# A fused attention and mixture-of-experts kernel: gate work of the last unit at lower steps of the first routed slot, and planning by one scan over one combined number

## The chip, the cores and the metric

The kernel runs on 1 core of one Trainium2 chip. The metric is the device time of one execution in microseconds (us). The engines are TensorE (PE), VectorE (DVE), ScalarE (ACT), GpSimd (POOL) and SyncE (SP), which here only issues transfers.

## The reference

Three stages run one after the other; the change touches the passage from the second to the third.

```python
x = attention(q, k, v, w_phi)                    # 4608 tokens x 512
h = x @ w_in; x1 = (h * cos(h)) @ w_out          # dense stage
logits = x1 @ w_gate + modality_bias[modality_id]
e_idx = argmax(logits, axis=1)                   # one of 8 experts per token
gate_w = softmax(logits)[token, e_idx]
for e in range(8):                               # routed stage
    mask = e_idx == e
    out[mask] = gate_w[mask, None] * (relu(x1[mask] @ w1[e]) @ w2[e])
```

## The kernel before

**Dense stage.** The 4608 tokens go in 9 units of 512, and a unit runs 16 steps. Every float32 operand is split in a high and a low part, and a product is three matmuls. For the last two units the result x1T (512 features by 512 tokens) is gated on TensorE: `logits(u,d)` splits a quarter d of x1T on DVE and POOL (x1h, x1l), and its returned function `pe` does two matmuls into `pl`; after the fourth quarter ACT copies `pl` out (lsb). `rows(u,c)` transposes 128 tokens (pr) and writes them to x1d in memory. `route1(u)` turns the logits (pt) into one-hot rows ob. `route2(u)` ranks every token within its expert (matmuls pk) and writes one record (token, weight) per token into the table `tab` by four scatters on POOL (L601), each of which waits for the one before. The table has a region of REG rows for each expert.

**Routed stage.** Tokens of one expert are worked off in slots of 256 (`body`). A slot needs its records (mrec, loaded by SP from `tab`, L713), its rows of x1 (xg, two gathers on POOL, L715), and its expert's weights: 8 loads of 512 KB into raw tiles (`fetch`, L690 and L691, on SP), each split in two casts by ACT (high part, L697) and two subtractions by DVE (low part, L698). `body(i)` has 12 steps: 4 steps of 24 matmuls mh, each followed by hh on ACT and hl on DVE, and 8 steps of 6 matmuls po, in two halves of 24. `finish` scales a half on ACT (o) and writes it out by an indirect transfer on POOL (L788). `prep(i)` transposes slot i's rows (px) and splits them to xT; `hooks` puts it behind step 9 of the slot before.

**The place of the change.** Slots 0 and 1 use the expert that has the most tokens before the last unit, so they can start before the last unit is routed. The rest of the gate work of unit 8 (the last) is put between the steps of slot 0, by the table given to `run`: after step n, its entries run. `order` then plans all later slots from the final counts: a slot's expert (ie), its offset in `tab` (io) and the numbers of full and half slots (ni), by small operations on one partition of DVE. SP reads ie and io into registers (L613, called by `load_e` and `load_off`) before it loads records and weights. `tokens(2)` is the load of slot 2's records and its gathers, `weights(8,12)` its first four weight loads (raw_8, raw_9, raw_10 and raw_0); the others are issued from the hooks of slot 1.

**What sets the order.** Each engine runs its instructions in one fixed order. A scheduler chooses it when the program is built, from the program's steps and its own estimates of durations; the table sets the program order, and the scheduler may move work of other tiles past it. SP's queue is in order as well: what stands behind the record load waits for it. Buffers are shared by tag: "row" turns among kvt, kvt and qt; "fr" is kt, "n" is qt.

The table before:

```python
    run(body(0,0),{0:[lambda:lg(0)(u)],1:[lambda:pe(u),lambda:lg(1)(u)],2:[lambda:pe(u),lambda:lg(2)(u)],3:[lambda:pe(u),lambda:lg(3)(u)],
             4:[lambda:rows(u,0)],5:[lambda:pe(u),lambda:rows(u,1)],6:[lambda:rows(u,2)],7:[lambda:rows(u,3),lambda:route1(u)],
             9:[lambda:route2(u)],10:[lambda:prep(1)],11:[order,lambda:tokens(2),lambda:load_e(2),lambda:load_e(3),lambda:weights(8,12)]})
```

Of the kernel before, what the change touches and what calls it, by code (L numbers as in the profile page):

```python
# [296 lines left out]
def gate_consts(tc, ctx, cpool, ps, ident, modality_id, modality_bias, w_gate, wgt):  # L297
    nc=tc.nc
    C={}
    with tc.tile_pool(name="g_tmp",bufs=1) as tp:  # L300
# [31 lines left out]

        sl=tp.tile([1,25],I32,name="sl"); nc.gpsimd.iota(sl,pattern=[[1,25]],base=0,channel_multiplier=0)
        slot=cpool.tile([1,25],F32,name="slot"); nc.vector.tensor_copy(slot,sl)

        tok=cpool.tile([P,4,9],I32,name="tok")
        nc.gpsimd.iota(tok[:,:,0:4],pattern=[[1152,4],[1,4]],base=0,channel_multiplier=4)
# [14 lines left out]
        nc.vector.tensor_tensor(bt,mf.unsqueeze(2).to_broadcast([P,36,8]),mb[:,1:2,:].to_broadcast([P,36,8]),ALU.mult)  # L352
        nc.vector.tensor_tensor(b0,mz.unsqueeze(2).to_broadcast([P,36,8]),mb[:,0:1,:].to_broadcast([P,36,8]),ALU.mult)
        nc.vector.tensor_tensor(bt,bt,b0,ALU.add)
    C.update(g1=g1,g2=g2,fold=fold,tri=tri,one=one,rev=rev,run=run,base=base,tok=tok,bt=bt,num=num,slot=slot,pool=cpool)
    return C


def moes(tc, ctx, consts, S, ps, ident, att, end_att, xt, w_in, w_out, x1d, tab, wgt, w1, w2, out):
# [10 lines left out]
    def xtile(tag,name,dt=F32R):  # L370
        if tag=="x1T": return late[0].tile([P,512],dt,tag="x1T",name=name,bufs=4)
        if tag=="row": return S(turn(("kvt","kvt","qt"),tag),name,dt)
        return S({"fr":"kt","n":"qt","gh":"kvh","gl":"kvl"}[tag],name,dt)
# [149 lines left out]
    lsb={}; pls={}  # L523
    def logits(u,d):

        h=xtile("row",f"x1h_{u}_{d}"); l=xtile("row",f"x1l_{u}_{d}")
        nc.vector.tensor_copy(h,x1T[u,d])
        nc.gpsimd.tensor_tensor(l,x1T[u,d],f32(h),ALU.subtract)
        def pe():
            if d==0: pls[u]=ms(f"pl_{u}")  # L530
            pl=pls[u]
            nc.tensor.matmul(pl[0:16,:],C["g1"][:,d,:],h,start=d==0,stop=False)
            nc.tensor.matmul(pl[0:16,:],C["g2"][:,d,:],l,start=False,stop=d==3)
            if d==3:
                t=xtile("row",f"lsb_{u}",F32)
                nc.scalar.copy(t[0:16,:],pl[0:16,:])
                lsb[u]=t[0:16,:]
        return pe
# [16 lines left out]
    def small(n,u,shape,dt=F32): return sb.tile(shape,dt,tag="s_"+n,name=f"{n}_{u}",bufs=1)  # L555
# [71 lines left out]
    def order():  # L627
# [4 lines left out]
        srt=small("srt",0,[1,8]); nc.vector.max(srt,t)  # L632
        ki=small("ki",0,[1,8],I32); nc.vector.tensor_copy(ki,srt)
        ei=small("ei",0,[1,8],I32); nc.vector.tensor_scalar(ei,ki,7,None,op0=ALU.bitwise_and)
        e=small("oe",0,[1,17]); nc.vector.memset(e[:,16:17],0.0)
        nc.vector.tensor_copy(e[:,0:8],ei); nc.vector.tensor_copy(e[:,8:16],ei)
        nc.vector.tensor_scalar(ki,ki,0xffff,None,op0=ALU.bitwise_and)
        n=small("on0",0,[1,16])
        for j,more in ((0,T//2-1),(1,T-1)):
# [1 line left out]
            nc.vector.tensor_scalar(kj,kj,11,None,op0=ALU.logical_shift_right)  # L641
            nc.vector.tensor_copy(n[:,8*j:8*j+8],kj)
        nc.vector.tensor_tensor(n[:,8:16],n[:,8:16],n[:,0:8],ALU.subtract)
        b=small("ob",0,[1,17]); nc.vector.tensor_scalar(b,e,float(REG),None,op0=ALU.mult)
        nc.vector.scalar_tensor_tensor(b[:,8:16],n[:,0:8],float(T),b[:,8:16],op0=ALU.mult,op1=ALU.add)
        end=n
        for i in (1,2,4,8):
            t2=small(f"on{i}",0,[1,16]); nc.vector.tensor_copy(t2[:,0:i],end[:,0:i])
            nc.vector.tensor_tensor(t2[:,i:16],end[:,i:16],end[:,0:16-i],ALU.add)
            end=t2  # L650
        de=small("de",0,[1,16]); nc.vector.tensor_tensor(de,e[:,1:17],e[:,0:16],ALU.subtract)
        do=small("do",0,[1,16]); nc.vector.tensor_tensor(do,b[:,1:17],b[:,0:16],ALU.subtract)
        nc.vector.scalar_tensor_tensor(do,n,-float(T),do,op0=ALU.mult,op1=ALU.add)
        ge=small("ge",0,[1,NS1,16])
        ie=small("ie",0,[1,NS1],I32); io=small("io",0,[1,NS1],I32)
        se=small("se",0,[1,NS1]); so=small("so",0,[1,NS1])
        for d_,s_ in ((de,se),(do,so)):
            nc.vector.tensor_tensor(ge,C["slot"].unsqueeze(2).to_broadcast([1,NS1,16]),end.unsqueeze(1).to_broadcast([1,NS1,16]),ALU.is_ge)
            nc.vector.tensor_tensor(ge,ge,d_.unsqueeze(1).to_broadcast([1,NS1,16]),ALU.mult)
            nc.vector.tensor_reduce(s_,ge,AX.X,ALU.add)  # L660
        nc.vector.tensor_scalar(ie,se,e[:,0:1],None,op0=ALU.add)
        nc.vector.scalar_tensor_tensor(so,C["slot"],float(T),so,op0=ALU.mult,op1=ALU.add)
        nc.vector.tensor_scalar(io,so,b[:,0:1],None,op0=ALU.add)

        ni=small("ni",0,[1,2+NSH],I32)
        nc.vector.tensor_copy(ni[:,0:1],end[:,7:8]); nc.vector.tensor_copy(ni[:,1:2],end[:,15:16])
# [122 lines left out]
    def run(steps,hooks):  # L789

        n=0
        for _ in steps:
            for f in hooks.get(n,()): f()
            n+=1
        for f in hooks.get("end",()): f()
# [4 lines left out]
    def lg(d):  # L800
        def f(u): pend.append(logits(u,d))
        return f
    def pe(u): pend.pop(0)()
# [52 lines left out]
    def tokens(i):  # L856
        if i<NS0+2: alloc_g(i)
        load_off(i); gather(i)
    def weights(m0,m1):
        for m in range(m0,m1): fetch(m)  # L860
    run(body(0,0),{0:[lambda:lg(0)(u)],1:[lambda:pe(u),lambda:lg(1)(u)],2:[lambda:pe(u),lambda:lg(2)(u)],3:[lambda:pe(u),lambda:lg(3)(u)],
             4:[lambda:rows(u,0)],5:[lambda:pe(u),lambda:rows(u,1)],6:[lambda:rows(u,2)],7:[lambda:rows(u,3),lambda:route1(u)],
             9:[lambda:route2(u)],10:[lambda:prep(1)],11:[order,lambda:tokens(2),lambda:load_e(2),lambda:load_e(3),lambda:weights(8,12)]})
    def hooks(i,steps):


# [117 lines left out]
```

## Time and profile before

| What | us |
|---|---|
| median of 3 runs (1785.21 to 1790.61) | 1786.19 |
| the profiled execution | 1787.86 |
| its span in the trace | 1786.2 |
| TensorE busy | 1721.5 (96%) |
| DVE busy | 1243.0 (70%) |
| ACT busy | 931.2 (52%) |
| POOL busy | 640.0 (36%) |

TensorE is busy in 96% of the span. The page's slices show where it isn't: in the first part of the span, in two short stretches between 1260 and 1350 us (the passage from the dense to the routed stage), and at the end. A wait of another engine costs nothing as long as TensorE has work. "At 1331.26" means 1331.26 us after the start of the span.

### The profile page before, as it was taken

To read this page: it belongs to the slowest core of one execution; us is meant where nothing else is said; L and a number is where in the kernel's file an instruction comes from. 1 tells how busy PE (TensorE), PEld (TensorE's weight loads), DVE (VectorE), ACT (ScalarE), POOL (GpSimd) and SP (SyncE) were. 2 spreads that over 40 slices of the span, in tenths; PEclk is the share of its full clock that TensorE was granted. 3 is DMA by queue.
4 is the path that set the end of the run, shared out by engine and by line. 5 is a ranking of instruction groups with operands and counts; after the bars stand their busy time and mean duration, and the time that the engine had idled before them with its cause. 6 is when DMAs were issued, how large, how long until landed. Compare 5 with 4: busy or idle time off the path is not lost. (4 is left out here: it accounts for less than half of the span.)

```text
span 1786.2 us, 27417 instructions
## 1 busy us (share of the span) xinstructions
PE 1721.5 (96%) x9818; PEld 1481.6 (83%) x9818; DVE 1243.0 (70%) x2366; ACT 931.2 (52%) x1694; POOL 640.0 (36%) x496
## 2 busy tenths in 40 slices
PE   8999999998889999999999999999889999999986
PEld 7999999997668888888888888888778999999975
DVE  6878877779896586868586868574547565666555
ACT  5777777776554343434343434343427555565555
POOL 0544544546654233434333333343322221111121
PEclk9999999999899999999999999999999999999998
DMA  6334333332332010101010101000329775766666
GB/s 177 101 112 125 90 100 105 87 95 98 119 112 78 12 36 12 36 12 36 12 36 13 36 13 36 13 1 24 118 83 389 236 236 198 258 220 222 221 222 221
DMA packets 144614, 194.37 MB, mean 109 GB/s; under 512 B 64967, under 2 KB 89671, under 8 KB 144466
## 3 DMA queue, kind: packets, MB, share of 16 engines
q1 hardware_dynamic: 136514, 170.93, 30.3%
q0 software_dynamic: 7952, 21.54, 3.6%
q8 instruction: 83, 1.36, 0.3%
q14 instruction: 65, 0.53, 0.1%
HBM read 162.70 MB, written 30.51 MB: 108 GB/s over the span
## 5 line engine op out<-in xcount | busy, mean ns | idle before, releaser
L455 PE MATMUL ph<-x,w 128*128 128x512 f32 x1728 | 427.9, 396 | 10.3 <-DVE fr L474 9.0
L455 PEld LDWEIGHTS ph<-x,w 128*128 128x128 f32 x1728 | 325.8, 190 | 88.3 <-DVE fr L474 12.2
L477 POOL TENSOR_TENSOR gl<-fr,gh 128x512 fp32r<-128x512 f32 x144 | 215.0, 1495 | 397.4 <-DVE gh L476 329.6
L698 DVE TENSOR_TENSOR m<-raw,m 128x512 fp32r<-128x512 f32 x336 | 219.2, 694 | 134.0 <-ACT m L697 131.8
L487 PE MATMUL acc<-w,gh 128*128 128x512 f32 x896 | 276.3, 390 | 0.0
L697 ACT CAST m<-raw 128x512 fp32r<-128x512 f32 x336 | 195.6, 618 | 70.8 <-PE mh L738 31.4
L468 ACT ACTIVATE n<-ph 128x512 int32<-128x512 f32 x144 | 85.8, 596 | 263.9 <-PE ph L455 260.9
L738 PEld LDWEIGHTS mh<-xT,m 128*128 128x128 f32 x1728 | 211.3, 193 | 4.9 <-ACT xT L724 2.3
L738 PE MATMUL mh<-xT,m 128*128 128x256 f32 x1728 | 212.5, 284 | 2.3 <-ACT xT L724 1.8
L487 PEld LDWEIGHTS acc<-w,gh 128*128 128x128 f32 x896 | 168.8, 188 | 35.0
L470 DVE SCALAR_TENSOR_TENSOR fr<-ph,n 128x512 f32<-128x512 f32 x144 | 99.1, 688 | 134.9 <-ACT n L468 114.6
L487 PE MATMUL acc<-w,gl 128*128 128x512 f32 x448 | 175.2, 392 | 6.8 <-POOL gl L477 6.8
L750 PE MATMUL po<-m,hh 128*128 128x512 f32 x576 | 181.2, 396 | 0.0
L517 DVE SCALAR_TENSOR_TENSOR junk<-x1T,wg 128x512 f32<-128x512 f32 x224 | 180.1, 804 | 0.0
L471 ACT ACTIVATE fr<-fr 128x512 f32<-128x512 f32 x144 | 91.1, 633 | 160.3 <-DVE fr L470 159.7
L168 PEld LDWEIGHTS kv<-v,ke 128*128 128x128 f32 (+1 forms) x1280 | 146.4, 191 | 13.0 <-issue 7.1
L168 PE MATMUL kv<-v,ke 128*128 128x65 f32 (+1 forms) x1280 | 152.0, 273 | 1.7 <-ACT ke L148 1.6
L474 DVE SCALAR_TENSOR_TENSOR fr<-fr,ph 128x512 f32<-128x512 f32 x144 | 98.6, 685 | 74.5 <-ACT fr L472 74.3
L788 POOL DMA_INDIRECT out_dram<-o,mrec x39 | 39.5, 1014 | 292.9 <-ACT o L787 253.4
L223 PE MATMUL pn<-qx,kvz 128*128 128x288 f32 x512 | 136.3, 409 | 3.2 <-DVE xo L230 3.0
L750 PEld LDWEIGHTS po<-m,hh 128*128 128x128 f32 x576 | 106.1, 190 | 20.2
L223 PEld LDWEIGHTS pn<-qx,kvz 128*128 128x128 f32 x512 | 92.6, 191 | 24.7 <-DVE xo L230 3.7
(210 smaller groups left out, 2940.8 us busy)
## 6 DMA issues: line engine op xcount, KB each, us to landing
raw<-in_moe_w_dram SPq DMA_DIRECT2D x179, 512.0 KB
xt<-xo SPq DMA_DIRECT2D x16, 576.0 KB
xr<-xt SPq DMA_DIRECT2D x36, 256.0 KB
raw_k<-in_k_dram SPq DMA_DIRECT2D x32, 256.0 KB
raw_q<-in_q_dram SPq DMA_DIRECT2D x32, 256.0 KB
v<-in_v_dram SPq DMA_DIRECT2D x64, 128.0 KB
st<-in_moe_w_in_dram SPq DMA_DIRECT2D x16, 512.0 KB
st<-in_moe_w_out_dram SPq DMA_DIRECT2D x16, 512.0 KB
```

Source lines behind the costliest of these rows:

```text
L168: nc.tensor.matmul(o,e[p0:p1,idx*256+s*F:idx*256+(s+1)*F],vh[p0:p1,h,cc,:],start=first and h==0 and s==0,stop=last,skip_group_check=True)
L223: nc.tensor.matmul(pn,kz[:,s,h*P:(h+1)*P],qx[:,h,s,su],start=s==0,stop=s==1)
L455: nc.tensor.matmul(ph,A[:,ws],xhl[u,d][k],start=n[0]==0,stop=n[0]==11); n[0]+=1
L470: nc.vector.scalar_tensor_tensor(g,ph,INV2PI,n,op0=ALU.mult,op1=ALU.subtract)
L474: nc.vector.scalar_tensor_tensor(g,g,-0.5,ph,op0=ALU.add,op1=ALU.mult)
L477: nc.gpsimd.tensor_tensor(gl,g,f32(gh),ALU.subtract)
L487: nc.tensor.matmul(accs[u][c],A[:,ws],B,start=(f==0 and k==0),stop=(f==NF-1 and k==2))
L517: return lambda: tc.keep_in_program_order(nc.vector.scalar_tensor_tensor(junk,x1T[u,c],1.0,wg[e],op0=ALU.mult,op1=ALU.mult,accum_out=lgs[u ...
L697: nc.scalar.copy(h,a)
L698: nc.vector.tensor_tensor(l,a,f32(h),ALU.subtract)
L738: nc.tensor.matmul(ph[:,f2*T:(f2+1)*T],A[:,ws],B[d//2][:,xs],start=n==0,stop=n==11); n+=1
L750: nc.tensor.matmul(po[c],A[:,ws],B,start=(f==0 and j==0),stop=(f==NF2-1 and j==2))
```

## The change

The gate work of unit 8 moves to lower steps: all four splits after step 0, all eight gate matmuls after step 2, `route1` after step 3 (before: 7), `route2` after step 6 (before: 9), `order` after step 7, and the record, expert and weight loads of slot 2 after step 8 (before: 11). Three of the four splits get buffers of the tags "fr" and "n". In `order`, the expert and the offset of a slot become one number (8 times the offset plus the expert), so that one compare, multiply and sum over 25 x 16 numbers gives both; a mask and a shift take them apart. The doubling steps of the running sum become one scan.

```diff
--- before.py
+++ after.py
@@ -332,6 +332,7 @@
 
         sl=tp.tile([1,25],I32,name="sl"); nc.gpsimd.iota(sl,pattern=[[1,25]],base=0,channel_multiplier=0)
         slot=cpool.tile([1,25],F32,name="slot"); nc.vector.tensor_copy(slot,sl)
+        ones=cpool.tile([1,16],F32,name="ones"); nc.vector.memset(ones,1.0)
 
         tok=cpool.tile([P,4,9],I32,name="tok")
         nc.gpsimd.iota(tok[:,:,0:4],pattern=[[1152,4],[1,4]],base=0,channel_multiplier=4)
@@ -352,7 +353,7 @@
         nc.vector.tensor_tensor(bt,mf.unsqueeze(2).to_broadcast([P,36,8]),mb[:,1:2,:].to_broadcast([P,36,8]),ALU.mult)
         nc.vector.tensor_tensor(b0,mz.unsqueeze(2).to_broadcast([P,36,8]),mb[:,0:1,:].to_broadcast([P,36,8]),ALU.mult)
         nc.vector.tensor_tensor(bt,bt,b0,ALU.add)
-    C.update(g1=g1,g2=g2,fold=fold,tri=tri,one=one,rev=rev,run=run,base=base,tok=tok,bt=bt,num=num,slot=slot,pool=cpool)
+    C.update(g1=g1,g2=g2,fold=fold,tri=tri,one=one,rev=rev,run=run,base=base,tok=tok,bt=bt,num=num,slot=slot,ones=ones,pool=cpool)
     return C
 
 
@@ -523,7 +524,8 @@
     lsb={}; pls={}
     def logits(u,d):
 
-        h=xtile("row",f"x1h_{u}_{d}"); l=xtile("row",f"x1l_{u}_{d}")
+        th,tl=("fr","n") if u==NU-1 and d<3 else ("row","row")
+        h=xtile(th,f"x1h_{u}_{d}"); l=xtile(tl,f"x1l_{u}_{d}")
         nc.vector.tensor_copy(h,x1T[u,d])
         nc.gpsimd.tensor_tensor(l,x1T[u,d],f32(h),ALU.subtract)
         def pe():
@@ -632,8 +634,6 @@
         srt=small("srt",0,[1,8]); nc.vector.max(srt,t)
         ki=small("ki",0,[1,8],I32); nc.vector.tensor_copy(ki,srt)
         ei=small("ei",0,[1,8],I32); nc.vector.tensor_scalar(ei,ki,7,None,op0=ALU.bitwise_and)
-        e=small("oe",0,[1,17]); nc.vector.memset(e[:,16:17],0.0)
-        nc.vector.tensor_copy(e[:,0:8],ei); nc.vector.tensor_copy(e[:,8:16],ei)
         nc.vector.tensor_scalar(ki,ki,0xffff,None,op0=ALU.bitwise_and)
         n=small("on0",0,[1,16])
         for j,more in ((0,T//2-1),(1,T-1)):
@@ -641,26 +641,22 @@
             nc.vector.tensor_scalar(kj,kj,11,None,op0=ALU.logical_shift_right)
             nc.vector.tensor_copy(n[:,8*j:8*j+8],kj)
         nc.vector.tensor_tensor(n[:,8:16],n[:,8:16],n[:,0:8],ALU.subtract)
-        b=small("ob",0,[1,17]); nc.vector.tensor_scalar(b,e,float(REG),None,op0=ALU.mult)
-        nc.vector.scalar_tensor_tensor(b[:,8:16],n[:,0:8],float(T),b[:,8:16],op0=ALU.mult,op1=ALU.add)
-        end=n
-        for i in (1,2,4,8):
-            t2=small(f"on{i}",0,[1,16]); nc.vector.tensor_copy(t2[:,0:i],end[:,0:i])
-            nc.vector.tensor_tensor(t2[:,i:16],end[:,i:16],end[:,0:16-i],ALU.add)
-            end=t2
-        de=small("de",0,[1,16]); nc.vector.tensor_tensor(de,e[:,1:17],e[:,0:16],ALU.subtract)
-        do=small("do",0,[1,16]); nc.vector.tensor_tensor(do,b[:,1:17],b[:,0:16],ALU.subtract)
-        nc.vector.scalar_tensor_tensor(do,n,-float(T),do,op0=ALU.mult,op1=ALU.add)
+
+        b=small("ob",0,[1,17]); nc.vector.memset(b[:,16:17],0.0)
+        nc.vector.tensor_scalar(b[:,0:8],ei,8.0*REG+1.0,None,op0=ALU.mult)
+        nc.vector.scalar_tensor_tensor(b[:,8:16],n[:,0:8],8.0*T,b[:,0:8],op0=ALU.mult,op1=ALU.add)
+        end=small("on1",0,[1,16])
+        nc.vector.tensor_tensor_scan(end,C["ones"],n,0.0,op0=ALU.mult,op1=ALU.add)
+        db=small("db",0,[1,16]); nc.vector.tensor_tensor(db,b[:,1:17],b[:,0:16],ALU.subtract)
+        nc.vector.scalar_tensor_tensor(db,n,-8.0*T,db,op0=ALU.mult,op1=ALU.add)
         ge=small("ge",0,[1,NS1,16])
-        ie=small("ie",0,[1,NS1],I32); io=small("io",0,[1,NS1],I32)
-        se=small("se",0,[1,NS1]); so=small("so",0,[1,NS1])
-        for d_,s_ in ((de,se),(do,so)):
-            nc.vector.tensor_tensor(ge,C["slot"].unsqueeze(2).to_broadcast([1,NS1,16]),end.unsqueeze(1).to_broadcast([1,NS1,16]),ALU.is_ge)
-            nc.vector.tensor_tensor(ge,ge,d_.unsqueeze(1).to_broadcast([1,NS1,16]),ALU.mult)
-            nc.vector.tensor_reduce(s_,ge,AX.X,ALU.add)
-        nc.vector.tensor_scalar(ie,se,e[:,0:1],None,op0=ALU.add)
-        nc.vector.scalar_tensor_tensor(so,C["slot"],float(T),so,op0=ALU.mult,op1=ALU.add)
-        nc.vector.tensor_scalar(io,so,b[:,0:1],None,op0=ALU.add)
+        nc.vector.tensor_tensor(ge,C["slot"].unsqueeze(2).to_broadcast([1,NS1,16]),end.unsqueeze(1).to_broadcast([1,NS1,16]),ALU.is_ge)
+        nc.vector.tensor_tensor(ge,ge,db.unsqueeze(1).to_broadcast([1,NS1,16]),ALU.mult)
+        sv=small("sv",0,[1,NS1+8])[:,0:NS1]; nc.vector.tensor_reduce(sv,ge,AX.X,ALU.add)
+        nc.vector.scalar_tensor_tensor(sv,C["slot"],8.0*T,sv,op0=ALU.mult,op1=ALU.add)
+        iv=small("iv",0,[1,NS1],I32); nc.vector.tensor_scalar(iv,sv,b[:,0:1],None,op0=ALU.add)
+        ie=small("ie",0,[1,NS1],I32); nc.vector.tensor_scalar(ie,iv,7,None,op0=ALU.bitwise_and)
+        io=small("io",0,[1,NS1],I32); nc.vector.tensor_scalar(io,iv,3,None,op0=ALU.logical_shift_right)
 
         ni=small("ni",0,[1,2+NSH],I32)
         nc.vector.tensor_copy(ni[:,0:1],end[:,7:8]); nc.vector.tensor_copy(ni[:,1:2],end[:,15:16])
@@ -858,9 +854,9 @@
         load_off(i); gather(i)
     def weights(m0,m1):
         for m in range(m0,m1): fetch(m)
-    run(body(0,0),{0:[lambda:lg(0)(u)],1:[lambda:pe(u),lambda:lg(1)(u)],2:[lambda:pe(u),lambda:lg(2)(u)],3:[lambda:pe(u),lambda:lg(3)(u)],
-             4:[lambda:rows(u,0)],5:[lambda:pe(u),lambda:rows(u,1)],6:[lambda:rows(u,2)],7:[lambda:rows(u,3),lambda:route1(u)],
-             9:[lambda:route2(u)],10:[lambda:prep(1)],11:[order,lambda:tokens(2),lambda:load_e(2),lambda:load_e(3),lambda:weights(8,12)]})
+    run(body(0,0),{0:[lambda:[lg(d)(u) for d in range(4)]],2:[lambda:[pe(u) for d in range(4)]],3:[lambda:route1(u)],
+             4:[lambda:rows(u,0)],5:[lambda:rows(u,1)],6:[lambda:route2(u),lambda:rows(u,2)],7:[lambda:rows(u,3),order],
+             8:[lambda:tokens(2),lambda:load_e(2),lambda:load_e(3),lambda:weights(8,12)],10:[lambda:prep(1)]})
     def hooks(i,steps):
 
 
```

Three places show how instructions move. The first is TensorE in slot 0, around the last step of mh (pl is the gate matmul, pr a transposition for x1d). Before:

```order
L738 MATMUL mh_0_3_12131<-xT_0_1_11985,m0_7_11797 128x256 x3
L532 MATMUL pl_8_12089<-x1h_8_2_12127,g1_591 16x512
L533 MATMUL pl_8_12089<-x1l_8_2_12128,g2_592 16x512
L750 MATMUL po_0_0_12166<-m1_0_11798,hh_0_0_12052 128x512 x2
L750 MATMUL po_0_0_12166<-m1_0_11798,hl_0_0_12053 128x512
L750 MATMUL po_0_0_12166<-m1_1_11799,hh_0_0_12052 128x512 x2
L750 MATMUL po_0_0_12166<-m1_1_11799,hl_0_0_12053 128x512
L542 MATMUL pr_8_0_12174<-ident_60,x1T_8_0_12012 128x128
```

Now:

```order
L534 MATMUL pl_8_12132<-x1h_8_0_12058,g1_591 16x512
L535 MATMUL pl_8_12132<-x1l_8_0_12059,g2_592 16x512
L534 MATMUL pl_8_12132<-x1h_8_1_12062,g1_591 16x512
L535 MATMUL pl_8_12132<-x1l_8_1_12063,g2_592 16x512
L534 MATMUL pl_8_12132<-x1h_8_2_12066,g1_591 16x512
L535 MATMUL pl_8_12132<-x1l_8_2_12067,g2_592 16x512
L534 MATMUL pl_8_12132<-x1h_8_3_12070,g1_591 16x512
L535 MATMUL pl_8_12132<-x1l_8_3_12071,g2_592 16x512
L734 MATMUL mh_0_3_12143<-xT_0_0_11986,m0_1_11793 128x256 x3
```

All eight gate matmuls now stand in a row ahead of the last step of mh; before, the third pair stood behind it and the fourth later still.

The second is POOL behind the last split x1l (tab is the scatter of records, out_0_dram a slot's result, xg a gather). Before:

```order
L528 TENSOR_TENSOR x1l_8_3_12163<-x1T_8_3_12018,x1h_8_3_12162 128x512
L788 DMA out_0_dram<-o_0_0_12220,mrec_0_11771 4608x512
L601 DMA tab_67<-rec_8_12257,pi_8_12294 38912x2 x2
L788 DMA out_0_dram<-o_0_1_12326,mrec_0_11771 4608x512
L601 DMA tab_67<-rec_8_12257,pi_8_12294 38912x2 x2
L715 DMA xg_2_0_12399<-x1d_66,mrec_2_12398 128x512
```

Now:

```order
L530 TENSOR_TENSOR x1l_8_3_12071<-x1T_8_3_12020,x1h_8_3_12070 128x512
L603 DMA tab_67<-rec_8_12196,pi_8_12257 38912x2
L784 DMA out_0_dram<-o_0_0_12277,mrec_0_11773 4608x512
L603 DMA tab_67<-rec_8_12196,pi_8_12257 38912x2 x3
L784 DMA out_0_dram<-o_0_1_12397,mrec_0_11773 4608x512
L711 DMA xg_2_0_12347<-x1d_66,mrec_2_12346 128x512
```

The first scatter now stands ahead of slot 0's first output write, and the second output write behind all four scatters.

The third is ACT from slot 1's first hh on (m2 are the split weights of slot 2's second product, raw the loaded ones, o a scaled result). Before:

```order
L740 ACTIVATE hh_1_0_12442<-mh_1_0_12417 128x512
L740 ACTIVATE hh_1_1_12492<-mh_1_1_12467 128x512
L740 ACTIVATE hh_1_2_12521<-mh_1_2_12496 128x512
L740 ACTIVATE hh_1_3_12550<-mh_1_3_12525 128x512
L697 CAST m2_0_11806<-raw_8_12024 128x512
L697 CAST m2_1_11807<-raw_8_12024 128x512
L697 CAST m2_2_11808<-raw_9_12025 128x512
L697 CAST m2_3_11809<-raw_9_12025 128x512
L697 CAST m2_4_11810<-raw_10_12026 128x512
L697 CAST m2_5_11811<-raw_10_12026 128x512
L697 CAST m2_6_11812<-raw_0_11782 128x512
L787 ACTIVATE o_1_0_12595<-po_1_0_12554,mrec_1_11777 128x512
```

Now:

```order
L736 ACTIVATE hh_1_0_12427<-mh_1_0_12402 128x512
L736 ACTIVATE hh_1_1_12477<-mh_1_1_12452 128x512
L693 CAST m2_0_11808<-raw_8_12026 128x512
L693 CAST m2_1_11809<-raw_8_12026 128x512
L693 CAST m2_2_11810<-raw_9_12027 128x512
L693 CAST m2_3_11811<-raw_9_12027 128x512
L736 ACTIVATE hh_1_2_12506<-mh_1_2_12481 128x512
L693 CAST m2_4_11812<-raw_10_12028 128x512
L693 CAST m2_5_11813<-raw_10_12028 128x512
L693 CAST m2_6_11814<-raw_0_11784 128x512
L736 ACTIVATE hh_1_3_12535<-mh_1_3_12510 128x512
```

hh_1_2 and hh_1_3 of slot 1 now stand behind casts of slot 2's weights. DVE has the same new order, with hl_1_2 and hl_1_3 behind the low parts of these casts.

## Rows read from the trace of the kernel before

**Rows 1.** Busy us by stretch: PE, PEld, DVE, ACT, POOL; clock, DMA, GB/s

```profile
1270.00:1275.00 5.00, 2.53 (x6) 2.05 (x7) 4.55 (x6) 4.50 (x8) 2.40 (x2) 0.70 1.02 369
...
1335.00:1340.00 5.00, 0.00 (x0) 0.00 (x0) 2.59 (x4) 2.63 (x5) 0.96 (x1) 0.68 1.04 370
1340.00:1345.00 5.00, 3.20 (x11) 2.72 (x12) 2.80 (x5) 3.35 (x7) 1.33 (x2) 0.50 1.05 396
1345.00:1350.00 5.00, 5.00 (x25) 4.29 (x25) 5.00 (x9) 4.95 (x11) 2.31 (x2) 0.79 1.04 393
```

**Rows 2.** Timeline of PE: start, us, engine, line, operation [idle before, releaser]

```profile
1340.48 0.48 PE L723 MATMUL px<-ident,xg 128*128 128x128 f32 x1 [7.92 <-DMA xg<-x1d,mrec]
...
1342.27 1.75 PE L723 MATMUL px<-ident,xg 128*128 128x128 f32 x7 [1.31 <-DMA xg<-x1d,mrec]
...
1348.09 11.78 PE L738 MATMUL mh<-xT,m 128*128 128x256 f32 x96
```

**Rows 3.** Timeline of POOL: the last unit's four scatters, an output write

```profile
1310.48 0.98 POOL L601 DMA_INDIRECT tab<-rec,pi  x1 [2.55 <-DVE ki L633]
1315.56 0.96 POOL L601 DMA_INDIRECT tab<-rec,pi  x1 [4.10 <-DMA tab<-rec,pi]
1316.82 0.98 POOL L788 DMA_INDIRECT out_dram<-o,mrec  x1 [0.30 <-issue]
1321.76 0.96 POOL L601 DMA_INDIRECT tab<-rec,pi  x1 [3.96 <-DMA tab<-rec,pi]
1326.52 0.96 POOL L601 DMA_INDIRECT tab<-rec,pi  x1 [3.79 <-DMA tab<-rec,pi]
```

**Rows 4.** Timeline of the SP queue: the load of slot 2's records

```profile
1331.26 0.39 SPq L713 DMA_DIRECT2D mrec<-tab  x1
```

**Rows 5.** Waits of the SP queue, 1290-1480: us in total, times, longest

```profile
SPq L613 <- DVE ie L661: 11.0, 1, 11.0
SPq L713 <- DMA tab<-rec,pi: 10.6, 1, 10.6
```

**Rows 6.** Timeline of PE and its weight loads in slots 0 and 1

```profile
1298.31 0.60 PE L542 MATMUL pr<-ident,x1T 128*128 128x128 f32 x4
...
1298.66 0.71 PE L750 MATMUL po<-m,hh 128*128 128x512 f32 x2
...
1308.63 0.12 PEld L587 LDWEIGHTS <-tri 128*128 128x128 bf16 x2 [0.26 <-DVE s L576]
...
1310.46 1.03 PE L723 MATMUL px<-ident,xg 128*128 128x128 f32 x8
...
1326.97 0.61 PE L750 MATMUL po<-m,hh 128*128 128x512 f32 x2
...
1327.65 0.61 PE L750 MATMUL po<-m,hh 128*128 128x512 f32 x2
```

**Rows 7.** Timeline of ACT: last hh of slot 1, then slot 2's casts

```profile
1324.42 0.60 ACT L740 ACTIVATE hh<-mh 128x512 fp32r<-128x512 f32 x1 [2.28 <-PE mh L738]
1335.92 1.14 ACT L697 CAST m<-raw 128x512 fp32r<-128x512 f32 x2 [10.90 <-DMA raw<-in_moe_w_dram]
1337.61 1.14 ACT L697 CAST m<-raw 128x512 fp32r<-128x512 f32 x2 [0.56 <-DMA raw<-in_moe_w_dram]
...
1342.44 0.62 ACT L697 CAST m<-raw 128x512 fp32r<-128x512 f32 x1 [1.65 <-DMA raw<-in_moe_w_dram]
1342.96 0.68 ACT L787 ACTIVATE o<-po,mrec 128x512 f32<-128x512 f32 x1
```

**Rows 8.** Timeline of DVE: last planning step; low part of raw_0's first cast

```profile
1319.90 0.22 DVE L663 TENSOR_SCALAR io<-so,ob 1x25 int32<-1x25 f32 x1
...
1343.09 0.69 DVE L698 TENSOR_TENSOR m<-raw,m 128x512 fp32r<-128x512 f32 x1 [1.50 <-ACT m L697]
```

**Rows 9.** Timeline of POOL in unit 7: first and last of its four scatters

```profile
1246.25 0.99 POOL L601 DMA_INDIRECT tab<-rec,pi  x1 [0.15 <-DVE kmi L620]
...
1258.53 0.96 POOL L601 DMA_INDIRECT tab<-rec,pi  x1 [2.97 <-DMA tab<-rec,pi]
```

## The prediction

> **What bounds the kernel now.** I read the busy time of the engines in stretches first. Outside the first routed slots TensorE is full, so only a stretch where it idles can give time back. The last such stretch before the steady routed slots is at 1332 to 1347 us: TensorE does no work in one whole 5 us stretch, and its granted clock is 0.50 (1.2 GHz) in the next [rows 1]. The timeline of PE shows what it waits for: the transposes px of slot 2 wait 7.92 us and once more 1.31 us for the gather of x1 rows, and slot 2 itself starts at 1348.09 [rows 2]. I followed the gather backwards. POOL sends the record table of the last unit in four scatters, each only after the one before has landed [rows 3]; SP loads slot 2's records right after the fourth, at 1331.26 [rows 4]; and the list of waits of SP says that this load waited 10.6 us for the table alone, long after the planning numbers were there [rows 5]. The weight loads of slot 2 stand behind that load on SP, so they too are counted from it. I call this moment M; it is 1331.26 before.
>
> **The change, step by step.** *Gate earlier.* Count back from the rank matmuls pk, which began at 1308.63 [rows 6]. Between their old and their new place lie 18 matmuls po at 0.227 us (three start 0.68 us after three others), two groups of four transposes at 0.35 us from start to next start, and one pair of gate matmuls, about the size of two po: 4.08 + 0.70 + 0.46 = 5.2 us; the wait of 0.26 us ahead of pk goes as well [rows 6], since ob is then ready before. So pk begins near 1303.1. From pk to the first scatter took 1.85 us [rows 3, 6], so the first scatter is at 1305.0, 5.5 us earlier. The eight gate matmuls in a row need all four splits x1l. These now have buffers of their own and no longer wait for a matmul, and POOL has nothing else to do there; I count no wait. Without that cover each microsecond late costs one in M.
>
> *Scatters.* The order on POOL also changes: before, an output write stood between scatters 2 and 3; now one stands between 1 and 2, another behind 4. The interval with an output write 1.3 us behind the scatter was 6.20 us; the other two intervals on POOL were 5.08 and 4.76, and scatter 4 to SP's load 4.74 [rows 3, 4]. I take 6.20 + 4.76 + 4.76 + 4.74 = 20.5 us, since SP waits for the landing and not for POOL; M is then 1325.4, 5.9 us earlier. Bounds: in unit 7, four scatters began within 12.28 us, 4.09 each [rows 9], which gives M = 1321.4; 6.20 for each gives 1329.8. The Trainium skill (DMA: Bandwidth & Descriptors, section "Two DMAs through the same engine are not ordered") says that descriptors of one queue on one engine start in order; by that a write behind a scatter should not hold it up, M would be 1.4 us earlier and the end too, 1783.7. The 6.20 row speaks against it.
>
> *Planning.* Of the two compare, multiply and sum groups one goes, the doubling steps become one scan, and a mask and a shift that split the combined number are added. From pk to the last planning step DVE took 1308.63 to 1320.12, other work included [rows 6, 8]. I cost all of it at nothing: SP's load still waited 10.6 us for the table after the numbers were there [rows 5]. Even at its old length, 11.5 us, planning that begins with pk at 1303.1 ends at 1314.6, 11 us before the new M. Only without that cover would the shorter planning count, with some part of the 11.5.
>
> *What is moved along.* SP has the same order of loads as before, so the loads come at the old distances from M: raw_9 at M + 6.35 and raw_0 at M + 11.18, read from ACT's casts, which began when the loads landed [rows 7]. Nothing else on SP is passed.
>
> *The new wait.* The order shows what the diff doesn't. Before, ACT had all four hh of slot 1 ahead of slot 2's casts and did the last at 1324.42, then idled 10.90 us for raw_8 [rows 7]. Now hh_1_2 stands behind the four casts of raw_8 and raw_9, and hh_1_3 behind those of raw_10 and half of raw_0; DVE is in the same order. TensorE needs hh_1_2 after only 12 of slot 1's 48 po. These began about 1324.1, just before the last hh, and 0.3 us of waiting is gone, so that is at 1324.1 - 0.3 + 2.7 = 1326.5. That ACT doesn't pass over a waiting cast can be seen before: the output o of slot 1's first half ran at 1342.96, right behind the cast that had waited for raw_0, though its matmuls had been done since about 1330 [rows 7]. The Trainium skill (TensorE: Matmul & The Clock Gate, section "Architectural detail: the array is 16× 32×32, not 1× 128×128") calls the queues of ACT and DVE strict FIFO, which the o row agrees with; it is the rule that speaks against this change. If they were not, rival E below would be the result.
>
> So TensorE's wait for the gather is exchanged for a wait for weights, with more matmuls still to do behind it. hh_1_2: 1325.4 + 6.35 + 1.14 + 0.60 = 1333.5, so PE idles some 7 us from 1326.5. hh_1_3: raw_0 lands at 1336.6, its cast takes 0.62 and hh 0.60; on DVE the low part of that cast comes 0.65 us behind the cast's start and takes 0.69 [rows 7, 8], and hl_1_3 of the same shape as much again: 1336.6 + 0.65 + 0.69 + 0.69 = 1338.6. From there: 4 po, 12 po, the transposes px (1.03 us at full clock for slot 1's eight [rows 6]), 12 po: 28 x 0.227 + 1.03 = 7.4, so 1346.0. The clock: in the stretch from 1270, where PE resumed at 1272.5, the granted clock is 0.70, so 1.2 GHz for some 3 us; after px at 1342.27 it was at that level until about 1347.1, 4.8 us [rows 1, 2]. A second, short idle ends at 1337.8; 1.2 GHz from there for 0.8 to 4.8 us costs 0 to 2.0 us, and I take 1.0 (about 3 us, as at 1272). **Slot 2 starts at 1347.0 instead of 1348.09: a gain of 1.1 us.**
>
> Is slot 2 ready then? Behind raw_0 five more loads of 512 KB and 512 KB of gathers must land; at 396 GB/s [rows 1] that is 7.9 us, 1344.5; then two casts (1.14) and xT's first cast (0.62, as a raw cast of its shape): 1346.3 on ACT, 1347.0 with DVE's 0.69 [rows 7, 8]. It just fits. From then on TensorE is full as before, so the difference is carried to the end. The profiled execution took 1787.86 us with a span of 1786.2, and the median of the timed runs is 1786.19; I put the difference on the median: 1786.19 - 1.1 = 1785.1.
>
> **The rivals.** *B, faster: the scatters go at unit 7's pace.* M = 1321.4, the end 4.1 us earlier still: 1781.0. For it: the pace of 4.09 [rows 9]; against it: all four intervals of this very unit were longer [rows 3]. *E, faster: the casts don't hold hh up.* Then PE reaches px at 1332 and waits for the gather, at M + 9.2 and M + 11.0 (from rows 2 and 4), until 1336.4; with 12 po and the clock it could start slot 2 at 1341, but the last weights of its first matmuls land and are split only near 1343.4: a gain of 4.7, 1781.5. The order of ACT speaks against it. *C, slower: the loads of slot 3 hold slot 2 up.* hh_2_0 now stands behind eight casts for slot 3, before behind two. Behind raw_0 eight loads and 1 MB of gathers must land for that, 13.2 us at the rate above, 1349.8; two casts, hh and hl (2.4 us) bring 1352.2, and PE needs that at 1352.7, after 48 matmuls mh of slot 2. So it decides from a landing after 1350.3, and each microsecond later costs one. With these loads 5 us late (at 285 GB/s, say) PE idles 4.5 us, and with the clock at half after it loses 2 more: 1786.19 - 1.1 + 6.5 = 1791.6. Against it: before, the casts for slot 3 found their data there. *D, no change of the gate's time:* the gate matmuls wait for POOL or DVE and the first scatter stays at 1310.48. Then M is 5.5 us later than reckoned, and 1.1 us gained becomes 4.4 lost: 1790.6.
>
> **How the numbers follow.** About 0.3% (5.4 us) is what a measurement of this kernel can tell from no change. Forecast A, the exchange of one wait for another, 0.74; B 0.08; E 0.06; C 0.07; D 0.05. Faster by over 0.3% (under 1780.8) are about half of B and E and the lower end of A, with the clock soon back and a short interval each: 0.10. Slower by over 0.3% (over 1791.6) are most of C and a little of D and A: 0.08. Within 0.3%: 0.82. The range goes from B's time, 1781.0, to 6.20 us for three more scatter intervals less a little (M at 1329): 1789.5.
>
> **What would show it.** In the changed profile: the first scatter near 1305 and the four intervals; SP's record load near 1325.4; the list of waits with po waiting for hh on PE, and px no longer waiting for the gather; ACT's hh of slot 1 broken into two early and two late ones at 1333 and 1337; slot 2's first mh near 1347. The forecast is wrong if hh_1_2 runs before 1330, if the record load is not 4 us or more earlier, or if TensorE idles again in slot 2.

## The result: slower, by work that the diff doesn't touch

The changed kernel takes 1799.43 us (median of 4 runs, 1797.05 to 1800.62), the kernel before 1786.51 beside it: a ratio of 1.0066, 95% interval 1.0054 to 1.0078. The forecast was 1785.1 within 1781.0 to 1789.5; the time lies outside, on the other side. The profiled execution took 1797.05 us, with a span of 1795.3, 9.1 more than before (the medians differ by 12.9); the readings below are of it. One execution of a later kernel (slot 1's hh first, again) took 4448.44 us, for a cause that isn't known, and is left out of that kernel's ratio.

The changed passage does about what was forecast. The loss is elsewhere: the first matmul of routed slot 0, which stands ahead of every moved step, begins at 1289.12 instead of 1282.10. Lining up the 9818 matmuls of both traces one by one shows where the time goes: +1.5 us by the end of the attention, +7.0 by the end of the dense stage, +6.6 where slot 3 begins, +9.5 at the last matmul. So it is lost bit by bit in all three stages, and none in the passage that was changed.

### The profile page after: what moved, and what is told of

Read it like the earlier page. It is cut to its first block, busy times and chain, and to the rows that moved or that the text cites. A ratio compares the mean times of both kernels' runs of the same rounds, so it can differ in the third digit from the quotient of the medians.

```text
span 1795.3 us, 27417 instructions
## 1 busy us (share of the span) xinstructions
PE 1732.0 (96%) x9818; PEld 1481.8 (83%) x9818; DVE 1238.0 (69%) x2355; ACT 931.7 (52%) x1694; POOL 641.4 (36%) x496
## 5 line engine op out<-in xcount | busy, mean ns | idle before, releaser
L746 PE MATMUL po<-m,hl 128*128 128x512 f32 x288 | 114.0, 396 | 0.0
```

The source lines that it names most:

```text
L746: nc.tensor.matmul(po[c],A[:,ws],B,start=(f==0 and j==0),stop=(f==NF2-1 and j==2))
```

## The profile after

TensorE's share of the span is the 96% of before, and its busy time is longer:

```profile
span 1795.3 us, 27417 instructions
PE 1732.0 (96%) x9818; PEld 1481.8 (83%) x9818; DVE 1238.0 (69%) x2355; ACT 931.7 (52%) x1694; POOL 641.4 (36%) x496
```

A full engine can still do less. This is the list of groups for PE between 700 and 1100 us, in the dense stage (line, operation, shapes, count; busy us, mean ns of one; idle before), of the changed kernel:

```profile
L456 PE MATMUL ph<-x,w 128*128 128x512 f32 x864 | 211.6, 393 | 0.2
L488 PE MATMUL acc<-w,gh 128*128 128x512 f32 x575 | 179.2, 392 | 0.0
L488 PE MATMUL acc<-w,gl 128*128 128x512 f32 x287 | 112.7, 393 | 0.0
```

Together 1726 matmuls in 400 us. The same list before has 1743, at 389 to 391 ns:

```profile
L455 PE MATMUL ph<-x,w 128*128 128x512 f32 x867 | 211.9, 391 | 0.2
L487 PE MATMUL acc<-w,gh 128*128 128x512 f32 x584 | 179.8, 389 | 0.0
L487 PE MATMUL acc<-w,gl 128*128 128x512 f32 x292 | 113.6, 389 | 0.0
```

The granted clock is 1.00 there in both. On POOL, the first scatter of one unit and of the fifth unit after it, in the changed kernel and then before:

```profile
671.90 1.46 POOL L603 DMA_INDIRECT tab<-rec,pi  x1 [0.18 <-issue]
...
1116.93 1.25 POOL L603 DMA_INDIRECT tab<-rec,pi  x1
```

```profile
669.80 1.45 POOL L601 DMA_INDIRECT tab<-rec,pi  x1 [0.18 <-issue]
...
1110.64 1.25 POOL L601 DMA_INDIRECT tab<-rec,pi  x1 [0.15 <-issue]
```

(1116.93 - 671.90) / 5 = 89.0 us per unit; before it was (1110.64 - 669.80) / 5 = 88.2. The rate isn't the same through a unit. In the timeline of PE of the changed kernel, twelve matmuls ph, and the start of what follows them, at two places of a unit:

```profile
683.30 2.88 PE L456 MATMUL ph<-x,w 128*128 128x512 f32 x12
686.02 0.62 PE L488 MATMUL acc<-w,gh 128*128 128x512 f32 x2
...
727.46 2.96 PE L456 MATMUL ph<-x,w 128*128 128x512 f32 x12
730.26 0.63 PE L488 MATMUL acc<-w,gh 128*128 128x512 f32 x2
```

The first twelve take 2.72 us, 226.7 ns from start to start; the second twelve 2.80, 233.3 ns. The second twelve before:

```profile
724.72 2.88 PE L455 MATMUL ph<-x,w 128*128 128x512 f32 x12
727.44 0.62 PE L487 MATMUL acc<-w,gh 128*128 128x512 f32 x2
```

There they take 2.72 us too. The matmuls acc around them change pace in the same way. Matching each matmul with its tiles tells the two kinds apart. A tile comes from a pool, a stretch of on-chip memory, and the pools lie one behind the other: the constants, the pool "shared", the small tiles, and the pool "late" (in the attention, other pools in its place). From start to start it is about 227 ns where the network's weight lies in the shared pool. Where it lies in "late" (output weights 7 to 15, input weights 11 to 15) most take 229 to 236 ns, 232 in the mean. The other operand is in the shared pool. In ph the weight is the operand that is loaded, in most acc the one that is streamed; both are slower. Before, it was about 227 ns for all.

What changed for the late tiles is their address in the built program. The new constant `ones` takes 64 bytes of every partition and moves the shared tiles up by 64; the small tiles of the planning shrank by 320, so everything behind them lies 256 lower. Before, shared and late tiles both begin 288 bytes past a multiple of 512; after, the shared ones begin at 352 and the late ones at 32: a distance that was 0 and is now 192, counted from the shared tiles up to the late ones, modulo 512.

The passage itself. On POOL and SP, the scatters and the record load (answers [rows 3, 4]):

```profile
1311.69 1.01 POOL L603 DMA_INDIRECT tab<-rec,pi  x1 [11.16 <-DVE ki L635]
1313.40 1.01 POOL L784 DMA_INDIRECT out_dram<-o,mrec  x1 [0.71 <-ACT o L783]
1315.96 0.96 POOL L603 DMA_INDIRECT tab<-rec,pi  x1 [1.55 <-DMA tab<-rec,pi]
1321.61 0.96 POOL L603 DMA_INDIRECT tab<-rec,pi  x1 [4.68 <-DMA tab<-rec,pi]
1326.66 0.96 POOL L603 DMA_INDIRECT tab<-rec,pi  x1 [4.10 <-DMA tab<-rec,pi]
```

```profile
1330.61 0.39 SPq L709 DMA_DIRECT2D mrec<-tab  x1
```

On ACT, the casts stand ahead of slot 1's last two hh, which run between them at 1338.30 and 1340.51 (answers [rows 7]):

```profile
1325.04 0.60 ACT L736 ACTIVATE hh<-mh 128x512 fp32r<-128x512 f32 x1 [2.28 <-PE mh L734]
1335.78 1.14 ACT L693 CAST m<-raw 128x512 fp32r<-128x512 f32 x2 [10.15 <-DMA raw<-in_moe_w_dram]
1337.26 1.14 ACT L693 CAST m<-raw 128x512 fp32r<-128x512 f32 x2 [0.34 <-DMA raw<-in_moe_w_dram]
1338.30 0.59 ACT L736 ACTIVATE hh<-mh 128x512 fp32r<-128x512 f32 x1
...
1340.51 0.59 ACT L736 ACTIVATE hh<-mh 128x512 fp32r<-128x512 f32 x1
```

On PE, the wait for hh has taken the place of the wait for the gather, and slot 2 then waits for its xT (answers [rows 2]):

```profile
1319.09 11.67 PE L734 MATMUL mh<-xT,m 128*128 128x256 f32 x96
...
1338.94 1.22 PE L746 MATMUL po<-m,hh 128*128 128x512 f32 x2 [5.41 <-ACT hh L736]
...
1352.13 0.39 PE L734 MATMUL mh<-xT,m 128*128 128x256 f32 x1 [1.80 <-ACT xT L720]
```

## Experiments: placing

Three theories for the rate. D: a matmul slows down when its two operands' addresses are at a distance that isn't free. P: it slows down when the late tiles themselves stand at a bad address. I: the new instructions or their order cost the rate. The first four kernels change no instruction's place on any engine; they only add unused bytes behind the small tiles (which moves the late tiles), or among the constants (which moves both):

```diff
-        h2=small("oh1",0,[1,NSH]); ...
+        h2=small("oh1",0,[1,NSH+80])[:,0:NSH]; ...
```

with 80 words here (the changed kernel, 320 bytes), 48 and 16 words for the kernel before. The second kernel has instead 48 words behind `slot` among the constants, lets two small tiles share the buffers of dead ones, and drops the padding of a third.

> The changed kernel with 320 unused bytes at the end of the small tiles, so that the late tiles (weights 7 to 15 of the dense stage, part of the routed weights) lie 352 bytes past a multiple of 512, as the shared tiles do in it; no instruction differs. Theory D (distance: a matmul slows down when the addresses of its two operands stand at different places within 512 bytes) and theory P (place: it slows down when the late tiles themselves stand 32 bytes past a multiple of 512): both 226.7 ns from matmul to matmul in the whole dense stage, 88.2 us per unit, about 1785 us, as forecast. Rival I (the new instructions or the new order cost the rate): stays at 89.0 us per unit and about 1799 us.

> The changed kernel with 192 unused bytes among the constants and 192 fewer bytes of small tiles (two planning tiles share a buffer, one loses its padding), so that shared and late tiles both lie 32 bytes past a multiple of 512. D: no distance, so 88.2 us per unit and about 1785 us. P: now the shared tiles are badly placed too and every matmul of the dense stage takes 233.3 ns, 384 x 6.6 ns = 2.5 us per unit over the 88.2, about 1808 us or more. I: 1799 us.

> The kernel before with 192 unused bytes at the end of the small tiles: shared tiles stay 288 bytes past a multiple of 512, late ones move to 480. The distance is then 192, as in the changed kernel. D: unit 89.0 us, about 1797 us. P: 480 is as good a place as 288 or 352, 88.2 us per unit and 1786 us. I: 1786 us.

> The kernel before with 64 unused bytes at the end of the small tiles: shared tiles at 288, late ones at 352, distance 64. D: slower than 1786 us, between 1788 and 1798 us as the smaller distance counts fully or in part. P and I: 1786 us.

Measured: with the late tiles put back 1785.41 us (ratio to before 0.9999, 0.9989 to 1.0008); with all at 32, 1785.53 (1.0001, 0.9992 to 1.0011); before with the late tiles up by 192, 1797.51 (1.0069, 1.0052 to 1.0086); up by 64, 1798.61 (1.0070, 1.0053 to 1.0086), a little over what D expected. The kernel before was at 1786.62 beside them. Sixty-four unused bytes thus make the kernel before as slow as the changed one, and 320 unused bytes take the whole loss out of the changed one. So I falls, and P falls with the second and the fourth kernel: late tiles at 32 are fast when the shared ones are at 32 too, and at 352, a good address for shared tiles, they are slow. The same twelve ph and the same five units in the changed kernel with its late tiles put back:

```profile
723.96 2.88 PE L456 MATMUL ph<-x,w 128*128 128x512 f32 x12
726.68 0.62 PE L488 MATMUL acc<-w,gh 128*128 128x512 f32 x2
```

```profile
669.04 1.45 POOL L603 DMA_INDIRECT tab<-rec,pi  x1 [0.19 <-issue]
...
1109.81 1.25 POOL L603 DMA_INDIRECT tab<-rec,pi  x1 [0.15 <-issue]
```

2.72 us again, and (1109.81 - 669.04) / 5 = 88.2 us per unit. The routed stage answers too. Groups of PE from 1420 to 1700 us, po of the changed kernel, and then of the one with its tiles put back:

```profile
L746 PE MATMUL po<-m,hh 128*128 128x512 f32 x378 | 119.6, 397 | 0.0
```

```profile
L746 PE MATMUL po<-m,hh 128*128 128x512 f32 x384 | 119.7, 393 | 0.0
```

The matmuls mh beside them, of 256 columns, take 283 ns in both.

Which distances are free was asked of three more, padded in the same way (16 and 72 words in the changed kernel, 32 in the kernel before):

> The changed kernel with 64 unused bytes behind the small tiles: shared tiles at 352, late ones at 96, distance 256 (half of 512). If only multiples of 512 are free: 89.0 us per unit and about 1798 us. If multiples of 256 are free: 88.2 us and 1785.4 us.

> The kernel before with 128 unused bytes behind the small tiles: shared tiles 288 bytes past a multiple of 512, late ones 416, distance 128. If every distance that is no multiple of 256 costs the same: 233 ns from matmul to matmul with a late weight, 89.0 us per unit, about 1798 us. If multiples of 128 are free: 226.7 ns and 1786 us.

> The changed kernel with 288 unused bytes behind the small tiles: shared tiles at 352, late ones at 320, distance 32. If every distance that is no multiple of 256 costs the same: 89.0 us per unit, about 1798 us. If small distances are free: 88.2 us and 1785.4 us.

With 256 between them 1786.91 us (1.0004, 0.9995 to 1.0014); with 128, 1795.77, and with 32, 1799.23 (one run each, before at 1786.96). Of one group of PE in the 400 us from 700, at distances of 256 and of 128:

```profile
L488 PE MATMUL acc<-w,gh 128*128 128x512 f32 x584 | 179.9, 389 | 0.0
```

```profile
L487 PE MATMUL acc<-w,gh 128*128 128x512 f32 x576 | 179.3, 392 | 0.0
```

| Late less shared, bytes modulo 512 | Kernels | ph and acc, 700 to 1100 us | us |
|---|---|---|---|
| 0 | before; changed +320; all at 32 | 1743; 1744; 1744 | 1786.5; 1785.41; 1785.53 |
| 256 | changed +64 | 1743 | 1786.91 |
| 64 | before +64 | 1726 | 1798.61 |
| 128 | before +128 | 1725 | 1795.77 |
| 192 | changed; before +192 | 1726; 1725 | 1799.43; 1797.51 |
| 480 | changed +288 | 1724 | 1799.23 |

For the weights of the dense stage the two multiples of 256 are free, and the other four distances cost about the same. One more run asked whether that holds for the projections of the attention, whose weights wph lie in a third pool:

```diff
-    wraw=ap.tile([P,2*F],F32,name="wraw",bufs=1)
+    wraw=ap.tile([P,2*F+16],F32,name="wraw",bufs=1)[:,0:2*F]
```

> The changed kernel with its late tiles put back (320 bytes) and 64 more unused bytes ahead of the projection's weights wph in the attention, so that these stand 256 bytes from the shared kT and qT instead of 192; the dense and routed stages are as with 320. The projections pj_q took 119.0 to 119.5 ns in the kernels with late tiles out of step and 115.2 to 115.5 in the others, with wph at a distance of 192 in these. If the distance of a matmul's own two operands rules there too: at most 115.2 ns. If wph has to stand at 192, for whatever reason: about 119 ns. The time moves by less than 2 us.

It doesn't: the best distance is another. From one matmul's start to the next, in the mean, pj_q took 119.6 ns with wph 256 bytes from the shared qT, and 114.9 with 192; the whole took 1788.69 us (one run), 3.3 more than without the 64 bytes, where less than 2 was expected. The padding of the other kernels moves wph too. Over all fourteen traces pj_q goes with the distance modulo 256: 114.8 to 115.2 ns at 192 (eight traces), 117.0 at 64, 118.0 at 160, 118.8 and 118.9 at 128, 119.3 and 119.6 at 0. In the changed kernel it is 128, and 432 matmuls at 3.8 ns more are 1.6 us, which fits the 1.5 lost in the attention. Which operand meets which there wasn't found out, so "a multiple of 256" is the finding for the 512-column matmuls with late weights, and not a rule.

## Experiments: the passage

With placing out of the way the two halves of the change were run alone, every tile in step. The first is the kernel before with the gate's new steps and buffers; the second has the new planning with the gate's old steps, and the 320 bytes.

> The kernel before with the gate's new steps and the new buffers of its splits, its old planning, and every tile where it stood before (shared and late tiles both 288 bytes past a multiple of 512). Theory D (the loss is the distance between operands, the gain is the gate's): 88.2 us per unit; first scatter, less the shift at the start of routed slot 0, 5 to 7 us earlier; SP's record load near 1322; slot 2 some 3 us earlier; about 1785 us, as the whole change with its tiles put back (1785.4). Rival I2 (the planning is what brings the rest): record load later than 1324 and 1786.5 us.

> The kernel before with the new planning alone and 320 unused bytes behind the small tiles, so that shared and late tiles both lie 352 bytes past a multiple of 512. D: the planning is hidden behind SP's wait for the record table, so first scatter, record load and slot 2 stay where they were before, within 0.5 us after the shift at slot 0, and 1786.5 us. I2: record load earlier by 1 us or more, 1785 us.

The third is the whole change with the 320 bytes, and slot 2's first casts kept behind slot 1's hh:

```diff
-            nc.scalar.copy(h,a)
-            nc.vector.tensor_tensor(l,a,f32(h),ALU.subtract)
+            c=[nc.scalar.copy(h,a)]
+            c.append(nc.vector.tensor_tensor(l,a,f32(h),ALU.subtract)); i==2 and which==1 and [tc.keep_in_program_order(x) for x in c]
```

> The changed kernel with its late tiles put back (320 bytes), and slot 2's first eight casts and their low parts pinned behind slot 1's hh and hl on ACT and DVE; SP, POOL and PE keep their order. Theory F (the exchange of waits costs, as forecast): TensorE no longer waits 4.6 us for hh_1_2, slot 2 starts 1 us or more earlier than the 1344.0 of the kernel with the tiles put back, and the time is 1783 to 1784.5 us. Rival L (slot 2's own weights set its start: loads at the DMA's full 392 GB/s from the record load on): the wait for hh is gone and the same time is lost ahead of px and slot 2, whose first matmul stays within 0.5 us of 1344; 1785 us.

> The kernel of the run with slot 1's hh first once more, in more rounds, since its interval (0.9982 to 1.0002) just held 1. Theory F (the exchange of waits costs 1 to 3 us): 1782.5 to 1784.5 us, interval below 1. If the 1783.95 was chance: 1785.4 us, as without the pins.

From the first mh of slot 1, the traces measure the passage free of what came before it (us); the last column counts from slot 0's first mh:

| Kernel | Median | Slot 1 to slot 2 | Slot 1 to slot 3 | Slot 0 to record load |
|---|---|---|---|---|
| before | 1786.5 | 35.38 | 58.81 | 49.16 |
| changed | 1799.43 | 33.05 | 59.05 | 41.49 |
| changed, tiles put back | 1785.41 | 32.43 | 58.17 | 40.62 |
| gate alone | 1785.87 | 32.29 | 56.43 | 41.00 |
| planning alone | 1786.42 | 34.17 | 59.50 | 46.87 |
| hh first | 1783.95 | 29.74 | 55.37 | 40.22 |
| hh first, again | 1785.28 | 30.47 | 56.12 | 43.64 |

Apart from the medians, each row is of one trace. The padded kernels say how far such a row can be trusted: six traces of the changed order (without the pins) give 32.2 to 33.1 and 58.0 to 59.1 us to slots 2 and 3, and four of the old order 35.0 to 35.5 and 58.7 to 59.2. To the record load it is 40.2 to 43.6 in eight traces (the two with pins among them), and 47.8 to 49.2 in the four.

Gate alone brings the record load to where the whole change has it, so that part is the gate's. Planning alone brings it 2.3 us earlier than in the trace of before, but only 0.9 earlier than in one of the other three of the old order, and SP waited 13.6 us for the table there:

```profile
SPq L708 <- DMA tab<-rec,pi: 13.6, 1, 13.6
```

So that planning counts isn't shown. Either half alone is enough to move casts ahead of slot 1's hh, and TensorE then waits for hh, with the gate alone and with the planning alone:

```profile
PE po L751 <- ACT hh L741: 5.0, 1, 5.0
PE po L745 <- ACT hh L735: 7.1, 1, 7.1
```

Neither can be told from no change in the medians (gate alone 1.0001, 0.9991 to 1.0011; planning alone 1.0002, 0.9993 to 1.0012).

In the kernel with the tiles put back slot 2 starts 35.38 - 32.43 = 2.95 us earlier, and 2.3 of that is gone by slot 3. The waits of PE from 1300 to 1360 us, and two stretches of the table of busy times (columns as in [rows 1]):

```profile
PE po L746 <- ACT hh L736: 4.6, 1, 4.6
PE mh L734 <- ACT xT L720: 1.5, 1, 1.5
PE mh L734 <- DVE xT L721: 0.5, 1, 0.5
```

```profile
1340.00:1345.00 5.00, 2.92 (x16) 2.12 (x15) 3.71 (x7) 3.44 (x7) 0.00 (x0) 1.00 1.05 401
1345.00:1350.00 5.00, 5.00 (x31) 5.00 (x31) 3.93 (x7) 3.06 (x6) 1.10 (x1) 0.66 1.03 394
```

The second stretch with the gate alone, where the two waits for xT are 0.8 and 0.5 us and the clock wasn't lowered behind them:

```profile
1345.00:1350.00 5.00, 5.00 (x44) 5.00 (x43) 4.89 (x9) 4.76 (x9) 1.02 (x1) 1.00 1.03 392
```

On ACT, with the tiles put back, the cast of xT runs right behind casts that waited for a load:

```profile
1341.40 1.14 ACT L693 CAST m<-raw 128x512 fp32r<-128x512 f32 x2 [1.45 <-DMA raw<-in_moe_w_dram]
1342.45 1.06 ACT L720 CAST xT<-px 128x512 fp32r<-128x512 f32 x2
```

So slot 2 runs into its own wait for xT, and most of what was won ahead of it is paid back in it: 0.5 us is the second of these waits, and the lower clock accounts for about 1.5, by an estimate from the matmuls (31 in 5 us, and 44). With hh first, the exchange of waits is undone. On ACT slot 1's last hh is done before the first cast, and on PE the waits for the gather are back, 1.69 and 1.57 us:

```profile
1321.59 0.60 ACT L736 ACTIVATE hh<-mh 128x512 fp32r<-128x512 f32 x1 [2.28 <-PE mh L734]
1325.27 1.14 ACT L693 CAST m<-raw 128x512 fp32r<-128x512 f32 x2 [3.08 <-DMA raw<-in_moe_w_dram]
```

```profile
1331.43 0.33 PE L719 MATMUL px<-ident,xg 128*128 128x128 f32 x1 [1.69 <-DMA xg<-x1d,mrec]
1333.33 1.20 PE L719 MATMUL px<-ident,xg 128*128 128x128 f32 x7 [1.57 <-DMA xg<-x1d,mrec]
```

Slot 2 starts 2.0 to 2.7 us earlier than without the pins, which speaks for theory F and against L: the casts did hold hh up. That this shortens the whole isn't shown. The time is 1783.95 and, again, 1785.28 us, and 1785.4 was what the repeat named for chance; the ratios to before are 0.9992 (0.9982 to 1.0002) and 0.9993 (0.9984 to 1.0002). Both point to a little over 1 us less than the kernel before, and neither interval excludes none. Only the 14 us and more below the changed kernel are clear.

## Why the prediction was wrong

The step that failed is the frame of the sum. "Outside the first routed slots TensorE is full, so only a stretch where it idles can give time back" is right for a gain, and it was read as if nothing could be lost there either; "From then on TensorE is full as before, so the difference is carried to the end" makes that a step. TensorE was full, and did 1726 matmuls where it had done 1743. No rival had a changed rate in it: the prediction took the same order of the dense stage for the same time, and didn't ask where the tiles lie, though the diff adds a constant, drops eight small tiles and adds three, one of them with a padding of eight words. With that one thing put back the kernel takes 1785.41 us. That this is close to the forecast 1785.1 is partly luck: the kernel before, at 1786.62 beside it, can't be told from it, so the gain of 1.1 us is neither shown nor refuted, and the terms behind it were not all right:

- **Gate earlier.** Forecast 5.5 us for the first scatter. Counted from slot 0's first mh it is 5.8 earlier in the changed kernel (1311.69 - 1289.12 = 22.57, before 28.38); the eight traces of the changed order give 22.4 to 24.9, the four of the old order 27.2 to 28.6, their medians 4.9 apart. About right. The 0.3 us that TensorE waits for the fourth split, whose buffer still is of the old kind, was not foreseen, and is small.
- **Scatters.** Forecast 6.20 + 4.76 + 4.76 + 4.74 = 20.5 us; measured 4.27 + 5.65 + 5.05 + 3.95 = 18.9, and 18.2 with the tiles put back. The interval with an output write 1.7 us behind its scatter is now 4.27. In all fourteen traces the interval between the second and the third scatter is the longest, 5.3 to 5.7 us without a write in it (nine traces with the gate's new steps) and 5.9 to 6.2 with it (five with the old ones). Between the medians that is 0.5 us, so most of the 1.4 by which 6.20 exceeds 4.76 was not that write's doing; what it was stays open. From the first scatter to the record load the nine traces take 17.7 to 19.1 us: the term was mis-sized by 1.4 to 2.8. The record load comes 6.5 us earlier between the medians of eight and four traces (7.7 in the changed kernel's own), forecast 5.9. The Trainium skill's rule (DMA: Bandwidth & Descriptors, section "Two DMAs through the same engine are not ordered") is that descriptors of one queue on one engine start in order, by which that write shouldn't hold the scatter up. The 4.27 agrees with it.
- **Planning** at nothing: no difference in the time that can be measured. Alone it also moves casts ahead of hh, as the gate alone does.
- **The new wait.** Right in kind: 5.41 us for hh (4.6 with the tiles put back), forecast 7, less because the load was earlier. That the casts hold hh up is shown by hh first, where TensorE doesn't wait for it and slot 2 starts 2 us and more earlier. The Trainium skill (TensorE: Matmul & The Clock Gate, section "Architectural detail: the array is 16× 32×32, not 1× 128×128") calls these queues strict FIFO, and this pair of runs agrees.
- **Slot 2** was to start 1.1 us earlier, and starts 2.3 to 3.0 earlier. "It just fits" was wrong: TensorE waits another 2.0 us there for xT (2.3 in the changed kernel), one of the forecast's own signs of being wrong, and slot 2 itself takes 2.3 us longer, by the second of these waits and the clock. From slot 1 to slot 3 that leaves 0.6 of the forecast's 1.1 with the tiles put back.
- **The rivals.** B's earlier record load came in part, and not its price, since loads, casts and clock follow. E is what hh first makes of the kernel: its 4.7 us at slot 2 were measured as 4.9 and 5.6, but not 1781.5 us, since slot 2 then takes 25.6 us to slot 3 and not 23.4 as before. C was not seen: TensorE doesn't wait in slot 2 for hh_2_0. D was not seen.

## What to carry to other kernels

A small tile that is added or dropped moves every tile allocated behind it, and a full TensorE can then be slower by 0.7% with not one instruction moved: when a change touches a pool, compare the addresses of matmul operands modulo 512 with those before, and put them back with unused bytes before the change is judged. In a trace such a loss shows as fewer matmuls in a stretch that is as busy, and as a drift ahead of the changed place; read first where the two traces begin to differ. A wait that is removed ahead of a load-bound stretch is given back in part: price the next wait, and the clock behind it. A row read from one trace is no measure of a microsecond: kernels with the same order of instructions, padded differently, say how far it scatters.

## What the runs showed of the hardware

- A 512-column matmul of the dense stage follows the one before after about 227 ns when the addresses of its two operands, weight and shared tile, differ by a multiple of 256 bytes, and mostly after 229 to 236 (2.72 and 2.80 us for twelve ph) when they don't; with four such distances (32 below, 64, 128 and 192 above a multiple of 256) the whole time is 0.5 to 0.7% longer, and not more for one of them than for another as far as single runs tell. The mechanism was not shown. For the 256-column projections another distance was better (114.9 ns at 192, 119.6 at 256), and the pace of mh, all of whose operands lie in the shared pool, didn't change (283 ns long in both).
- The Trainium skill (SBUF — State Buffer, section "SBUF: two separate sides") says that only a port pair shared by two other engines causes contention among the engines, and that TensorE never waits on anyone. In the rows above TensorE's matmuls idle for 0.2 us in 400 of the dense stage, so no wait shows here either, and yet those with badly placed tiles follow one another up to 3% more slowly. The measurement decides: where the operands lie counts. Whether anything contends there was not shown.
